# Order and size of the loads in the last stage of a long-convolution and mixture-of-experts kernel: x requested ahead of z, z in two halves, the last z stores on ScalarE's queue

## The chip, the cores and the metric

The kernel runs on one core of a Trainium2 chip. The metric is the device time of the whole program in microseconds (us), which is better when lower. A core has TensorE (PE, with its weight loads shown apart as PEld), VectorE (DVE), ScalarE (ACT), GpSimd (POOL) and SyncE (SP), each with its own instruction stream, and 16 DMA engines that they share. SP does no arithmetic here: it waits on semaphores and issues most of the DMAs, strictly in program order.

## The reference

The reference is a gated long convolution followed by a sparse layer of experts:

```python
h_filt = (np.maximum(pos_emb @ w1, 0) @ w2) * exp(-0.01 * pos)[:, None]
u = x * v
y = irfft(rfft(u, 2S) * rfft(h_filt, 2S), 2S)[:, :S]      # causal convolution, S = 11456, 4 batches, 128 channels
t = (x * y).reshape(B * S, D)                             # 45824 rows of 128
do_compute = t @ w_skip > 0
e = argmax(t @ w_gate);  g = softmax(t @ w_gate)[e]       # 8 experts
out = t;  out[do_compute] += g * (relu(t @ w1[e]) @ w2[e])   # hidden size 1024
```

## The kernel before, in words

The convolution is done as a two-step Fourier transform with 60 x 64 points, with the sequence cut into three blocks (`NB = 3`) and the 128 channels into four quarters of 32. There are three stages.

- `first_phase` multiplies x by v, computes the filter, and does the first half of the forward transform. Its result goes to DRAM (`x1d`, `x1f`).
- `freq_phase` reads it back, multiplies by the filter in the frequency domain, does the first half of the inverse transform, and stores the result in DRAM as `zd`. Its `store()` (line 425) issues two DMAs of 384 KB for each finished z tile, from SP (line 429). It is called once in each turn of the loop, and once more after the loop (line 481) for the last tile.
- `out_phase`, the last stage, has 32 chunks (`NCH = 32`) of 3 blocks, so 96 blocks. For a chunk it needs a tile `zt` with its part of `zd` (1440 KB, all three blocks of it; there are `ZB = 2` such tiles), and for each block a tile `ox` with the same rows of x (256 KB, three tiles, `ZT = 3`). `product` (line 1060) does the second half of the inverse transform for one block: matmuls of `zt` into the PSUM tile `y` (line 1068; the first pair of matmuls reads rows 0 to 3 of `zt`, the second pair rows 4 to 7), then a DVE multiplication of `y` with `ox` into `xm` (line 1069). There is one `y` buffer, so the matmuls of a block wait for the multiplication of the block before.

After its product each block goes through steps that lag behind: transposes of `xm` on PE (`turn`), the scores (`score`, `score2`), and, per chunk, the choice of the expert, counts, ranks and a list of the rows of each expert that a DMA writes to DRAM (`write`, line 1197). The block itself is stored to `out` seven steps after its product (`store`, line 1073). From about the ninth chunk on, the instructions of the first expert units (`early_slots`) are mixed in: GpSimd reads the lists and gathers rows by indirect DMAs (lines 657 and 691), PE multiplies them with the experts' weights, and GpSimd scatters the results (line 762). After the last chunk `late_slots` does the remaining units, with almost no other DMA work.

What sets the order of the work is a table written out by hand (lines 1269 to 1294): one step for each block, and in it functions sorted by a rank. Chunk 0 has steps 0 to 2, chunk 1 steps 4 to 6, chunk 2 steps 7 to 9, and from there on each chunk follows the last without a gap. Each engine gets its instructions in that order at build time, and waits only on semaphores. Within a step, a list write has rank -3, the product rank 0, and the store of an earlier block rank 9. So SP's stream in a steady chunk is: block 0 - ox, out; block 1 - list, ox, out; block 2 - zt, ox, out. An ox that is asked for at block q is the one for block q + 2, and the zt asked for at block 2 of chunk ch is the one for chunk ch + 2, which takes the tile that chunk ch has just finished with.

The change touches `store` of the second stage (lines 425 to 430 and 481), `load_z` (1046), the first loads of the last stage (1205 to 1209) and `produced` (1262), which calls the loads after each product.

Of the kernel before, what the change touches and what calls it, by code (L numbers as in the profile page):

```python
# [10 lines left out]
F32 = mybir.dt.float32  # L11
# [10 lines left out]
NB = 3  # L22
K1, N2 = 60, 64
L = K1 * N2
H2 = N2 // 2
NS = NB * B
N = L * NS
NP = 4
DH = D // NP
# [16 lines left out]
KS = 4  # L46
# [7 lines left out]
ZT = 3  # L54
ZB = 2
# [265 lines left out]
def freq_phase(tc, nc, i, fi, zd, c3, spare, loads):  # L321
# [9 lines left out]
    with (  # L331
# [90 lines left out]
                step()  # L422
            return back

        def store():
            while done_z:
                h, k, z = done_z.pop()
                for p in range(2):
                    nc.sync.dma_start(zd[p, h, :, :, KS * k:KS * k + KS].rearrange("m c k d -> (m c) k d"),
                                      z[p * 64:(p + 1) * 64].rearrange("n k s d -> n k (s d)"))  # L430

        LAG = 1
# [16 lines left out]
        for n in range(ALL + LAG):  # L449
# [17 lines left out]
            back(0)  # L467
            begin(n + 1, 0)
            store()
            if n < ALL:  # L470
                half(1)
# [5 lines left out]
            if n < ALL:  # L477
                nc.gpsimd.tensor_tensor(y[:, 1:], y[:, 1:], p1, ALU.add)  # L478
                nc.gpsimd.tensor_tensor(y[:, 2:], y[:, 2:], p2, ALU.add)  # L479
            back(2)  # L480
        store()


class Experts:
# [515 lines left out]
def out_phase(tc, i, out, zd, ex, consts):  # L1000
# [3 lines left out]
    nc = tc.nc  # L1004
    NT = NS
    NCH = H2
    with (
# [3 lines left out]
      with (  # L1011
# [21 lines left out]
        zs = zd.rearrange("p h m c k w -> m (c k) (p h) w")  # L1033
        c4s, xms, zx, zts, lgs = {}, {}, {}, {}, {}

        def load_x(q):

            ch, blk = divmod(q, NB)
            if blk == 0 and ch % C4 == 0:
                c4s[ch // C4] = ob.tile([2 * K1, C4, 2, 64], F32, name="c4", bufs=2)  # L1040
                nc.sync.dma_start(c4s[ch // C4].rearrange("p a b c -> p (a b c)"), i["c4"][ch // C4])
            x = ob.tile([128, NP, B, DH], F32, name="ox", bufs=ZT)
            nc.sync.dma_start(x, i["xo"][ch, blk])
            return x

        def load_z(ch):
            if ch < NCH:
                zts[ch] = ob.tile([2 * K1, 2 * NP, NS * DH], F32, name="zt", bufs=ZB)
                nc.sync.dma_start(zts[ch], zs[ch])

        def load(q, x=None):

            ch, blk = divmod(q, NB)
            if q >= NB * NCH:
                return
            if x is None:
                x = load_x(q)
            zx[q] = zts[ch][:, :, blk * BW:(blk + 1) * BW], x

        def product(ch, blk):  # L1060
            z, x = zx.pop(NB * ch + blk)
            if blk == 0:
                xms[ch] = ob.tile([128, NS, W], F32, name="xm", bufs=XM)
            xm = xms[ch]
            s = slice(blk * B, (blk + 1) * B)
            y = opy.tile([128, NP, B, DH], F32, name="y")
            for p in range(2):
                nc.tensor.matmul(y[p * 64:(p + 1) * 64], c4s[ch // C4][:, ch % C4, p, :], z[:, NP * p:NP * (p + 1)], start=True, stop=True)  # L1068
            nc.vector.tensor_tensor(xm[:, s, 0:D].rearrange("p b (h d) -> p h b d", h=NP), y, x, ALU.mult)  # L1069

        def store(ch, blk):
            s = slice(blk * B, (blk + 1) * B)
            ex.store_rows(nc.sync.dma_start(out[ch][:, s], xms[ch][:, s]), ch)
            if blk == NB - 1:
                del xms[ch]
# [127 lines left out]
            base += n * u  # L1203
        work = ex.early_slots(eb, ob, eps, bank[2])
        ahead = [load_x(q) for q in range(ZT - 1)]
        for ch in range(ZB):
            load_z(ch)
        for q, x in enumerate(ahead):
            load(q, x)
        tables = []  # L1210
# [50 lines left out]

        def produced(ch, blk):
            product(ch, blk)
            if blk == NB - 1:
                load_z(ch + ZB)
            load(NB * ch + blk + ZT - 1)


        first = lambda ch: START[ch] if ch < len(START) else START[-1] + NB * (ch - len(START) + 1)
# [1 line left out]
        for ch in range(NCH):  # L1271
            for blk in range(NB):
                for lag, rank, f in ((0, 0, produced), (1, 4, turn), (2, 4.9, score), (3, 2, score2), (STORE, 9, store)):
                    steps.setdefault(first(ch) + blk + lag, []).append((rank, f, (ch, blk)))
            for lag, order, f in (
                    (6, 3, choose), (7, 1, exp), (7, 4.5, count), (7, 6, counted), (7, 6, gate), (8, 4.4, total),
                    (9, -2.5, even), (9, 0.5, spreadcounts), (9, 4.5, ranks),
                    (10, -2, routed), (11, 3, spread), (12, 4.5, collect), (13, -3, write)):
                steps.setdefault(first(ch) + lag, []).append((order, f, (ch,)))
# [27 lines left out]
def program(tc, i, out):  # L1307
# [5 lines left out]
    with tc.tile_pool(name="mc", bufs=1) as mc:  # L1313
        wf = mc.tile([128, 2 * E * F], F32, name="wf")
        fi = First(nc, i, x1d, x1f, mc, wf)
        spare = wf[:, fi.used:]
        c3 = mc.tile([128, 2, 128], F32, name="c3")
        first_phase(tc, fi)
        nc.scalar.dma_start(c3, i["c3"])
        later = {}  # L1320

        def prepare():

            later["ex"] = Experts(tc, i, out, lists, mc, wf)
            yield
            later["consts"] = out_consts(nc, i, mc)
            for e in range(E):
                if e % 2 == 0:
                    yield
                later["ex"].weights(e, 0)  # L1330

            for e in range(E):
                if e != 1:
                    yield
                later["ex"].weights(e, 1)
        freq_phase(tc, nc, i, fi, zd, c3, spare, prepare())
        out_phase(tc, i, out, zd, later["ex"], later["consts"])
# [53 lines left out]
```

## Time and profile before

| What | Value |
|---|---|
| Time, median of 3 runs | 1851.17 us (1851.14 to 1859.37) |
| The profiled execution's own time | 1847.63 us |
| Its span | 1845.8 us |
| Mean granted TensorE clock over the span | 0.928 of full |
| PE busy over the span | 1613.2 us (87%) |
| `zt` loads | 32 DMAs of 1440 KB |
| `ox` loads | 96 DMAs of 256 KB |
| `out` stores of blocks | 96 DMAs of 258 KB |

The span is the time from the first to the last instruction of one profiled execution. A row of a waits view reads: the engine and line that stood idle, what ended the idle time, the sum in us, how often, and the longest. A row of a windows view reads: the stretch in us from the start of the span, its length, then for each engine the busy us and the instructions, the granted TensorE clock, the mean busy share of the 16 DMA engines, and GB/s. The time that packets overlap on one DMA engine counts twice, so that share can go a little over 1. A row of a timeline reads: start, length, engine, line, operation, out<-in, count, and in brackets the idle time of the engine before it with what ended it; rows of SP are the issues of DMAs (several of one line in a row are merged), not their transfers.

### The profile page before, as it was taken

The numbers are of one execution on the slowest core, as the hardware profiler recorded it, in microseconds if no ns is written. First come the engines' busy times: TensorE is split into PE (matmuls) and PEld (weight loads), VectorE is DVE, ScalarE is ACT, GpSimd is POOL, SyncE is SP. The second block draws the span as 40 slices with busy tenths as digits, with TensorE's granted clock in tenths as the row PEclk, the third lists the DMA queues.
The fourth block names the chain that finished last, engine by engine and source line by source line (L and its number), as shares of the span: only waits on it lengthen the run. The fifth ranks groups of instructions, "written<-read, shape, count | busy, mean of one in ns | idle before, by whom it ended". The sixth has DMA issues, their size and how long they took to land. (4 is left out here: it accounts for less than half of the span.)

```text
span 1845.8 us, 26677 instructions
## 1 busy us (share of the span) xinstructions
PE 1613.2 (87%) x8528; PEld 1002.9 (54%) x8528; DVE 1194.7 (65%) x2521; ACT 831.1 (45%) x1740; POOL 1025.5 (56%) x667
## 2 busy tenths in 40 slices
PE   6968999999999999566887968999869988899897
PEld 2533333344334444222565756666657766778896
DVE  1316777777777999436774845676656645577775
ACT  3543545444455444122443534444425534455564
POOL 1115888888887788200455243234466666666674
PEclk9987999999999999787898989999889889899899
DMA  9999999999998798789986876887211111111110
GB/s 240 324 334 280 357 346 306 346 330 304 347 318 271 225 344 229 166 196 232 220 196 159 216 179 167 207 220 194 72 25 24 34 38 37 35 36 34 31 34 19
DMA packets 209385, 353.97 MB, mean 192 GB/s; under 512 B 55146, under 2 KB 157884, under 8 KB 209244
## 3 DMA queue, kind: packets, MB, share of 16 engines
q1 hardware_dynamic: 190332, 312.99, 58.6%
q0 software_dynamic: 18144, 38.67, 7.5%
q8 instruction: 69, 1.13, 0.3%
q10 hardware_dynamic: 768, 0.59, 0.1%
q14 instruction: 72, 0.59, 0.1%
HBM read 209.12 MB, written 144.02 MB: 191 GB/s over the span
## 5 line engine op out<-in xcount | busy, mean ns | idle before, releaser
L762 POOL DMA_INDIRECT out<-o,ids x186 | 206.0, 1107 | 316.0 <-DVE o L768 254.1
L418 PE MATMUL zps<-y,c 128*128 128x512 f32 x720 | 336.6, 597 | 1.8 <-POOL y L478 1.4
L478 POOL TENSOR_TENSOR y<-y,p 128x2048 f32<-128x2048 f32 x60 | 271.9, 4532 | 65.6 <-DVE p L407 65.1
L691 POOL DMA_INDIRECT xt<-out,ids x186 | 201.7, 1084 | 96.6 <-issue 53.3
L866 DVE SCALAR_TENSOR_TENSOR hh<-hp,hh 128x1024 fp32r<-128x1024 f32 x128 | 155.9, 1218 | 124.8 <-ACT hh L865 66.0
L418 PEld LDWEIGHTS zps<-y,c 128*128 128x128 f32 x720 | 134.5, 190 | 171.2 <-issue 154.2
L407 DVE TENSOR_TENSOR p<-xp,g 128x1024 f32<-128x1024 f32 x240 | 217.2, 945 | 0.0
L407 DVE TENSOR_TENSOR y<-xp,g 128x1536 f32<-128x1536 f32 x120 | 210.7, 1756 | 4.1
L657 POOL DMA_INDIRECT ids<-lists,at x93 | 102.8, 1106 | 158.7 <-DVE at L652 131.2
L865 ACT ACTIVATE hh<-hp 128x1024 fp32r<-128x1024 f32 x128 | 132.0, 1032 | 121.4 <-PE hp L758 60.2
L419 ACT COPY z<-zps 128x512 f32<-128x512 f32 x180 | 105.6, 587 | 167.4 <-PE zps L418 162.9
L1068 PE MATMUL y<-zt,c 120*64 120x512 f32 x384 | 117.0, 691 | 51.1 <-DVE xm L1069 24.5
L733 DVE TENSOR_TENSOR ws<-wf,ws 128x1024 fp32r<-128x1024 f32 x113 | 137.6, 1218 | 16.2 <-issue 9.8
L1069 DVE TENSOR_TENSOR xm<-y,ox 128x512 f32<-128x512 f32 x96 | 66.1, 689 | 126.1 <-PE y L1068 53.8
L756 PE MATMUL hp<-hl,ws 128*128 128x512 f32 (+1 forms) x336 | 127.7, 380 | 19.5 <-issue 10.7
L479 POOL TENSOR_TENSOR y<-y,p 128x1024 f32<-128x1024 f32 x60 | 141.7, 2362 | 4.7
L218 ACT COPY wf<-ps 120x384 f32<-120x384 f32 x256 | 110.0, 482 | 70.1 <-PE ps L216 70.1
L216 PE MATMUL ps<-wf,c 60*120 60x384 f32 x512 | 126.0, 563 | 13.1 <-POOL wf L199 7.2
L828 PEld LDWEIGHTS bank<-wd,h 128*128 128x128 f32 x928 | 116.8, 205 | 34.0 <-issue 34.0
L828 PE MATMUL bank<-wd,h 128*128 128x128 f32 x928 | 127.4, 294 | 0.4 <-issue 0.4
L387 PE MATMUL xp<-x,wf 128*128 128x480 f32 x256 | 120.7, 596 | 5.5 <-issue 3.8
L199 POOL TENSOR_TENSOR wf<-wf 124x768 f32<-124x768 f32 x48 | 87.3, 1818 | 63.7 <-DMA wf<-xv 33.6
(188 smaller groups left out, 3160.8 us busy)
## 6 DMA issues: line engine op xcount, KB each, us to landing
wf<-xv SPq DMA_DIRECT2D x128, 360.0 KB
x1d<-wf SPq DMA_DIRECT2D x64, 720.0 KB
x<-x1d SPq DMA_DIRECT2D x60, 768.0 KB
zd<-z SPq DMA_DIRECT2D x120, 384.0 KB
zt<-zd SPq DMA_DIRECT2D x32, 1440.0 KB
out<-xm SPq DMA_DIRECT2D x96, 258.0 KB
ox<-xo SPq DMA_DIRECT2D x96, 256.0 KB
x1f<-fx POOLq DMA_DIRECT2D x16, 720.0 KB
```

Of the source, the lines that this page charges most:

```text
L216: nc.tensor.matmul(ps[p], self.c1[rows], u[rows, q * RUN:(q + 1) * RUN], start=True, stop=True)
L407: nc.vector.tensor_tensor(o[:, :, :, j * KH:(j + 1) * KH].rearrange("p s a k b d -> p (s a) k b d"), x[:, None].broadcast_to([128, m, KH, ...
L418: nc.tensor.matmul(zps, c3[:, a, :], y[:, blk, a], start=(a == 0), stop=(a == 1))
L478: nc.gpsimd.tensor_tensor(y[:, 1:], y[:, 1:], p1, ALU.add)
L479: nc.gpsimd.tensor_tensor(y[:, 2:], y[:, 2:], p2, ALU.add)
L691: ins = nc.gpsimd.indirect_dma_start(out=xt[:, j], out_offset=None, in_=self.rows[0:have], in_offset=bass.IndirectOffsetOnAxis(ap=ids[:, j ...
L733: eng.tensor_tensor(w[:, 1], src[:, ds(self.where(eng, tb), F)], w[:, 0].bitcast(F32), ALU.subtract)
L756: nc.tensor.matmul(hp, w[:, 0, c], hl[:, 0], start=True, stop=False)
L762: ins = nc.gpsimd.indirect_dma_start(out=self.rows, out_offset=bass.IndirectOffsetOnAxis(ap=ids[:, j:j + 1], axis=0), in_=o, in_offset=Non ...
L828: nc.tensor.matmul(bank[:, j * D:(j + 1) * D], h[f // 2][:, f % 2, j * 128:(j + 1) * 128], wd[s][:, f * D:(f + 1) * D], start=(f == 0), st ...
L865: nc.scalar.activation(h[:, 0], hp, AF.Relu)
L866: nc.vector.scalar_tensor_tensor(h[:, 1], hp, 0.0, h[:, 0].bitcast(F32), ALU.max, ALU.subtract)
```

## The change

Three things change.

- After the product of a block, the ox of block q + 2 is now asked for first, and zt after it.
- A zt load is issued as two DMAs of 720 KB, rows 0 to 3 and rows 4 to 7 of the tile. The first half for chunk ch + 2 is asked for at block 2 of chunk ch, where the whole was; the second half at block 0 of chunk ch + 1, one block later. At the start only chunk 0's halves are asked for before the first product; both halves of chunk 1 follow at block 0 of chunk 0, behind the third ox.
- The store after the loop of the second stage, two DMAs, is issued by ScalarE instead of SP.

```diff
-        def store():
+        def store(eng=nc.sync):
             while done_z:
                 h, k, z = done_z.pop()
                 for p in range(2):
-                    nc.sync.dma_start(zd[p, h, :, :, KS * k:KS * k + KS].rearrange("m c k d -> (m c) k d"),
+                    eng.dma_start(zd[p, h, :, :, KS * k:KS * k + KS].rearrange("m c k d -> (m c) k d"),
                                       z[p * 64:(p + 1) * 64].rearrange("n k s d -> n k (s d)"))
...
-        store()
+        store(nc.scalar)
...
-        def load_z(ch):
+        def load_z(ch, p):
+
             if ch < NCH:
-                zts[ch] = ob.tile([2 * K1, 2 * NP, NS * DH], F32, name="zt", bufs=ZB)
-                nc.sync.dma_start(zts[ch], zs[ch])
+                if p == 0:
+                    zts[ch] = ob.tile([2 * K1, 2 * NP, NS * DH], F32, name="zt", bufs=ZB)
+                rows = slice(p * NP, p * NP + NP)
+                nc.sync.dma_start(zts[ch][:, rows], zs[ch][:, rows])
...
-        for ch in range(ZB):
-            load_z(ch)
+        for p in range(2):
+            load_z(0, p)
...
             product(ch, blk)
+            load(NB * ch + blk + ZT - 1)
+
             if blk == NB - 1:
-                load_z(ch + ZB)
-            load(NB * ch + blk + ZT - 1)
+                load_z(ch + ZB, 0)
+            elif blk == 0:
+                if ch == 0:
+                    load_z(1, 0)
+                load_z(ch + 1, 1)
```

## The prediction

> **What bounds the kernel now.** I read the stretches of the span first, then who waited for whom, then the timelines of SP and DVE where the waits lie. The last stage by stretches:
>
> ```profile
> core 0: us, PE busy (x) PEld busy (x) DVE busy (x) ACT busy (x) POOL busy (x), PEclk, DMA share, GB/s
> 764.00:794.50 30.50, 13.87 (x71) 5.06 (x71) 4.10 (x7) 3.51 (x10) 0.00 (x0) 0.72 0.94 194
> 794.50:808.50 14.00, 8.56 (x55) 3.61 (x54) 4.90 (x17) 3.44 (x12) 0.00 (x0) 0.74 0.86 199
> 808.50:822.50 14.00, 8.63 (x57) 3.75 (x54) 7.05 (x21) 3.07 (x11) 0.00 (x0) 0.74 0.84 191
> 822.50:836.50 14.00, 8.46 (x68) 4.08 (x67) 6.35 (x25) 3.46 (x12) 0.00 (x0) 0.74 0.96 237
> 836.50:851.00 14.50, 9.05 (x72) 4.33 (x71) 9.04 (x36) 3.53 (x12) 0.00 (x0) 0.74 0.93 221
> 851.00:864.50 13.50, 9.42 (x88) 4.68 (x90) 10.62 (x48) 3.56 (x12) 0.00 (x0) 0.88 0.92 227
> 864.50:878.50 14.00, 9.18 (x75) 4.35 (x74) 9.47 (x46) 3.46 (x12) 1.25 (x2) 0.74 0.98 228
> 878.50:895.00 16.50, 12.12 (x94) 6.03 (x92) 11.16 (x48) 5.07 (x15) 7.54 (x6) 0.71 0.81 192
> ...
> 910.00:1304.00 394.00, 339.07 (x2914) 248.88 (x2912) 245.51 (x907) 176.62 (x426) 159.75 (x150) 0.94 0.78 191
> 1304.00:1400.00 96.00, 71.89 (x522) 61.70 (x521) 59.91 (x235) 36.93 (x63) 59.39 (x55) 0.84 0.14 37
> 1400.00:1838.00 438.00, 395.03 (x2199) 341.54 (x2197) 290.43 (x421) 229.16 (x282) 279.52 (x251) 0.94 0.13 33
> ```
>
> Until about 895 us no engine is near full: a chunk of about 14 us has some 9 us of PE, at a clock of 0.74, while the DMA share is 0.81 to 0.98. From 910 to 1304 it is the reverse: PE is busy 339 of 394 us at a clock of 0.94. The change moves loads, so its effect lies before 895 if anywhere. Whether loads are waited for there:
>
> ```profile
> DVE xm L1069 <- DMA ox<-xo: 40.0, 10, 6.4
> ```
>
> ```profile
> DVE xm L1069 <- DMA ox<-xo: 4.6, 4, 3.2
> ```
>
> The first row is of 773 to 912 us, the second of 912 to 1310. So the multiplication waits for x about once per chunk, some 4 us each time, and hardly ever afterwards. Why it waits, from SP and DVE:
>
> ```profile
> 793.86 0.34 SPq L1049 DMA_DIRECT2D zt<-zd  x1
> 794.29 0.96 SPq L1043 DMA_DIRECT2D ox<-xo  x2
> ```
>
> ```profile
> 804.79 0.69 DVE L1069 TENSOR_TENSOR xm<-y,ox 128x512 f32<-128x512 f32 x1 [6.44 <-DMA ox<-xo]
> ```
>
> The 256 KB of x are asked for 0.43 us after 1440 KB of z, and are used 10.5 us later. And the DMA engines then run dry, because the next z is asked for only after a product that was itself held up:
>
> ```profile
> 758.50:762.50 4.00, 0.00 (x0) 0.00 (x0) 0.00 (x0) 0.00 (x0) 0.00 (x0) 0.55 0.94 226
> 762.50:764.50 2.00, 0.00 (x0) 0.00 (x0) 0.00 (x0) 0.00 (x0) 0.00 (x0) 0.50 0.86 286
> ...
> 772.00:779.50 7.50, 5.35 (x14) 1.63 (x16) 1.38 (x2) 0.32 (x1) 0.00 (x0) 0.51 1.06 203
> ...
> 792.50:794.50 2.00, 2.00 (x8) 0.83 (x8) 0.64 (x2) 0.00 (x0) 0.00 (x0) 0.64 0.02 8
> 794.50:796.00 1.50, 1.50 (x12) 0.50 (x12) 1.33 (x7) 1.01 (x3) 0.00 (x0) 0.50 0.54 118
> 796.00:802.50 6.50, 4.10 (x36) 1.75 (x32) 1.67 (x5) 1.94 (x7) 0.00 (x0) 0.96 1.10 213
> 802.50:806.50 4.00, 0.97 (x4) 0.29 (x4) 1.21 (x5) 0.30 (x1) 0.00 (x0) 0.60 0.98 295
> 806.50:808.50 2.00, 2.00 (x9) 1.06 (x6) 0.69 (x1) 0.19 (x1) 0.00 (x0) 0.50 0.07 25
> ```
>
> Read 792.5 to 808.5 as one chunk: 2 us empty, a slow start, z at a share of 1.10, x and out at 0.98, then empty again. **So the bound before 895 is the DMA queue together with a loop: x behind z delays the product, and the late product delays the next z.**
>
> **The change, part by part.**
>
> *Order and halves.* No byte is added: 1440 KB of z, three ox and three out per chunk remain. With x ahead, the last two products of a chunk no longer stand behind a whole z; each x has at most one half ahead of it. While one z tile is being used, both halves of the next are already queued, with x and out between, so the queue holds work when the next product comes. I therefore price the stretch by the queue alone. Its work is the sum of length times share: 30.5 x 0.94 + 14 x 0.86 + 14 x 0.84 + 14 x 0.96 + 14.5 x 0.93 + 13.5 x 0.92 + 14 x 0.98 + 16.5 x 0.81 = 118.9 us, in 131 us. A queue that stays full has a share of 0.98 (x and out, 802.5 to 806.5) to 1.05 (6.5 us at 1.10 with 4 us at 0.98). That gives 121.3 or 113.2 us: a gain of 9.7 to 17.8 us. I take 1.02: 116.6 us, **14.4 us less**. The eight rows cover about nine chunks, so a chunk would take some 13 us. PE's 9 and DVE's 4 to 11 us per chunk fit in that; the ox waits that remain cost nothing extra, since the queue is what they wait for.
>
> *The last of these chunks.* Part of the hole in 878.5 to 895 is not made by x:
>
> ```profile
> 888.89 0.77 PE L745 MATMUL mh<-ident,xt 128*128 128x128 f32 x2 [4.38 <-DMA xt<-out,ids]
> ```
>
> This is the first gather of an expert unit, a chain of indirect DMAs. At 1.02 the row has 16.5 - 13.4/1.02 = 3.4 us of hole; I keep half of it: **1.7 us back** (bounds 0 and 3.4).
>
> *Price of a second DMA per z.* SP's extra issue is 0.34 us, and SP stands idle, in the mean, 7.5 and 4.4 us before issues in block 1 of a chunk:
>
> ```profile
> SPq L1197 <- DVE sel L1163: 172.9, 23, 13.5
> SPq L1073 <- DVE xm L1128: 88.8, 20, 9.8
> ```
>
> On the queue, the two 384 KB stores of zd back to back (758.5 to 762.5) lack 0.06 x 4 = 0.24 us of a full share, their start included; from below, two z DMAs one behind the other (772 to 779.5) show no hole at all. Nine extra DMAs in the stretch: 0 to 2.2 us, taken as **1 us**; later the queue has room (0.78). Below nothing is possible only as in the second rival.
>
> A rule speaks against this part. The Trainium skill (DMA: Bandwidth & Descriptors, "Rules for kernel authors") wants 1 MiB or more per DMA for full bandwidth and says that two transfers to disjoint partition halves only serialize. The halves here lie side by side in the same partitions, yet both are under 1 MiB. Its "Anatomy of one DMA" fits a fixed 2.0 us to each DMA of the GpSimd path; nine of these one after the other would be an estimated 18 us and turn the sum into a loss. The row of 772 to 779.5, with a share of 1.06, shows no such pause between queued DMAs, so I do not follow it.
>
> *The second wait.* The second pair of matmuls of a chunk's first product now waits for a half of its own:
>
> ```profile
> L1068 PEldq EVENT_SEMAPHORE  x31: 51/51/51, 773.2 to 1288.7; - x31
> ```
>
> 51 ns, on the path in the some 22 of 32 chunks after 910: **1.1 us**. Behind it on PE stand that block's product and the transposes of the one before. It should find its half there: that was asked for three blocks earlier, and with 22 chunks in the 394 us a chunk takes 17.9 us.
>
> *The start.*
>
> ```profile
> 756.92 0.59 ACT L419 COPY z<-zps 128x512 f32<-128x512 f32 x1 [1.84 <-PE zps L418]
> 757.53 1.24 SPq L429 DMA_DIRECT2D zd<-z  x2
> 758.90 1.03 SPq L1041 DMA_DIRECT2D c<-c  x1
> 759.98 2.03 SPq L1043 DMA_DIRECT2D ox<-xo  x2
> 762.87 0.96 SPq L1049 DMA_DIRECT2D zt<-zd  x2
> 773.31 1.98 PE L1068 MATMUL y<-zt,c 120*64 120x512 f32 x4 [16.43 <-DMA zt<-zd]
> 779.18 0.59 ACT L1083 COPY xT<-tp 128x512 f32<-128x512 f32 x1 [21.68 <-PE tp L1081]
> ```
>
> SP waits for the last copy of z, stores it, and only then loads c4 and two ox; z must wait for the stores to land in any case. With the stores on ScalarE, c4 and the two ox (2 us, 762.5 to 764.5) can go before them, if their buffers are free, which no row shows. ScalarE's two issues (1.24 us on SP) stand in an idle time of 21.68 us; without that cover they would cost 1.24 us. The first pair of matmuls can start on the first half. Bounds: 0 and 2 + 2 = 4 us (both matmul pairs, 1.98, out of the way); I take **1 us gained**, near the lower end.
>
> *After 895.* The order of every engine is fixed and PE is the bound, so all later work moves with the stretch: no part is given back by rule. PE still stands idle 55 of 394 us there, in waits that the change does not touch but shifts, so 4 us either way may come of it.
>
> **Sum:** 14.4 - 1.7 - 1 - 1.1 + 1 = 11.6, so 12 us. The profiled execution took 1847.63 us (span 1845.8 and 1.8 around it) and would take 1836. It stands 3.5 us under the median of the runs, 1851.17, so I forecast **1839 us**, with 1831 to 1845 as this case's own range.
>
> **The rivals.**
>
> 1. *Fixed price per half.* The slow start in 794.5 to 796 (1.5 us at 0.54) costs 0.7 us. If each half pays it, two per chunk and nine chunks are 12.6 us less the 6.3 us paid now: gain 12 - 6 = 6 us, **1845 us**. For it: the slow start itself. Against it: the full share between two queued z. (The Trainium skill's fixed cost, above, would side with this rival.)
>
> 2. *More than the queue's sum.* The upper bounds hold: 17.8 us, 4 us at the start, no price of halves, no gather wait: about 22 us, **1829 us**. For it: the 40.0 us of waits are far above the sum. A gather, too, waits for a landing:
>
> ```profile
> 890.76 1.00 POOL L691 DMA_INDIRECT xt<-out,ids  x1 [7.67 <-DMA ids<-lists,at]
> ```
>
> If that is time behind a z, a half would shorten it. (By the Trainium skill, DMA: Bandwidth & Descriptors, "Queues, rings and completion order", an engine serves its queues in turn, a packet of up to 64 descriptors at a time, which would let a gather in between halves.) Against it: the share of 0.98 for x and out.
>
> 3. *The order does not get onto the queue.* SP's 7.5 and 4.4 us of idle time in block 1 come ahead of an x, and the holes stay. If the queue empties meanwhile, nothing is gained: **1851 us**. Against it: with both halves asked for just before block 1, some 8 us of work are queued then.
>
> 4. *Slower: the second half comes late.* It is asked for one block later than now. If, after 910, PE waits for it at each of 22 chunks, the 12 us are used up at 0.55 us per chunk, and at 1 us per chunk the kernel takes 1839 + 22 = **1861 us**. It decides once SP's hold and the queue together exceed the three blocks, 17.9 us. For it: the longest holds, 13.5 and 9.8 us. Against it: they come after the request in SP's order, and the queue is at 0.78.
>
> **How the numbers follow.** Forecast 0.52; more than the sum 0.20; fixed price 0.11; no new order 0.10; slower 0.07. A measurement of this kernel can tell about 0.5%, 9.3 us, from no change: faster is under 1841.9, slower over 1860.4. Faster: 0.40 of the forecast, 0.20, and 0.04 of the fixed price, 0.64. Slower 0.07, the rest 0.29. For the range I leave out what lies above 1852 (0.09) and below 1828 (0.09).
>
> **What would show it.** Right: between 773 and 905 the waits of line 1069 for ox shrink to well under 15 us, no 2 us windows with a share near 0 are left, a chunk takes about 13 us, the first expert unit's transposes, at 888.89, come near 877, and 910 to 1304 keeps its length. Wrong: holes of the same size (third rival), z windows with a share well under 1 (first), PE waits for zt after 910 (fourth), or a stretch after 895 that has grown by what was saved before it.

## The result

The changed kernel takes 1839.2 us (median of 12 runs, 1832.06 to 1848.6), the kernel before in the same comparison 1858.62 us (12 runs, 1851.14 to 1871.92). The ratio is 0.9905, with a 95% interval of 0.9881 to 0.9929, so 13 to 22 us of 1858.62 are gained, in the middle 17.7 us. That is more than the 0.5% which a measurement of this kernel can tell.

Of the two profiled executions, the one of before (1847.63 us) lies below all its 12 runs and the one of after (1840.31 us, span 1838.5) near its median. This pair shows only 7.3 us between them, so stages are compared one by one below.

The last stage of the changed kernel, in stretches (the columns are those of the prediction's first fence):

```profile
core 0: us, PE busy (x) PEld busy (x) DVE busy (x) ACT busy (x) POOL busy (x), PEclk, DMA share, GB/s
788.00:800.00 12.00, 9.38 (x62) 4.06 (x63) 5.61 (x17) 3.84 (x13) 0.00 (x0) 0.86 1.06 241
...
836.00:848.00 12.00, 9.78 (x59) 4.50 (x61) 7.98 (x43) 2.62 (x9) 0.00 (x0) 0.56 1.02 282
...
860.00:878.00 18.00, 11.22 (x87) 6.01 (x86) 12.75 (x54) 5.11 (x15) 6.01 (x6) 0.69 0.93 234
878.00:895.00 17.00, 15.57 (x145) 11.44 (x144) 11.22 (x42) 7.70 (x19) 6.33 (x7) 0.99 0.83 209
910.00:1296.00 386.00, 333.79 (x2826) 245.68 (x2826) 239.30 (x879) 170.34 (x414) 146.25 (x138) 0.92 0.74 185
```

The DMA share is 0.93 to 1.06 in these rows up to 878. Cut into windows of 2 us, 776 to 878 has a lowest share of 0.41, once, where before had windows of 0.02 and 0.07.

The waits of the changed kernel between 765 and 915 us, where before had 40.0 us for ox:

```profile
PE y L1071 <- DMA zt<-zd: 13.8, 4, 10.7
...
PE y L1071 <- DMA c<-c: 7.3, 2, 4.8
...
DVE xm L1072 <- DMA ox<-xo: 2.9, 3, 1.6
```

The wait for x is gone, from 40.0 to 2.9 us. Beside it stand PE's waits for z (10.7 of the 13.8 us are the first load) and, new, for c4, a small table that SP loads for two chunks at a time. What they cost is seen in the time of a chunk. Six chunks, from the first product of chunk 2 to that of chunk 8, first in before, then in after:

```profile
797.00:882.00 85.00, 54.30 (x409) 25.50 (x410) 48.78 (x195) 20.66 (x72) 4.23 (x3) 0.76 0.92 217
```

```profile
795.30:864.00 68.70, 54.89 (x418) 25.91 (x418) 48.84 (x194) 21.17 (x73) 1.73 (x2) 0.82 1.03 264
```

14.2 us per chunk became 11.45, with the same PE, DVE and ACT work in both, and 264 in place of 217 GB/s. This measure, six chunks from product to product, is used for all kernels below.

The start and the first expert, from the timeline of after:

```profile
756.11 1.74 SPq L1043 DMA_DIRECT2D ox<-xo  x2
...
760.26 0.59 ACT L419 COPY z<-zps 128x512 f32<-128x512 f32 x1 [1.84 <-PE zps L418]
760.88 1.15 ACTq L429 DMA_DIRECT2D zd<-z  x2
...
770.96 1.94 PE L1071 MATMUL y<-zt,c 120*64 120x512 f32 x2 [10.74 <-DMA zt<-zd]
...
776.52 0.69 DVE L1072 TENSOR_TENSOR xm<-y,ox 128x512 f32<-128x512 f32 x1 [17.13 <-PE y L1071]
...
872.20 1.04 PE L745 MATMUL mh<-ident,xt 128*128 128x128 f32 x2 [6.17 <-DMA xt<-out,ids]
```

SP asks for x at 756.11, ahead of the stores of z, and PE starts on the first half alone. The last copy of z (line 419), which the change does not touch, comes 3.3 us later in this execution than in before (760.26 against 756.92), so I measure from it. To the first multiplication it takes 16.26 us, where before took 775.38 - 756.92 = 18.46 us.

### The profile page after: what moved, and what is told of

The parts are those of the page before. It is cut to its first block, busy times and chain, and to the rows that moved or that the text cites. A ratio compares the mean times of both kernels' runs of the same rounds, so it can differ in the third digit from the quotient of the medians.

```text
span 1838.5 us, 26706 instructions
## 1 busy us (share of the span) xinstructions
PE 1614.4 (88%) x8528; PEld 1004.1 (55%) x8528; DVE 1195.8 (65%) x2521; ACT 831.1 (45%) x1740; POOL 1023.8 (56%) x667
## 5 line engine op out<-in xcount | busy, mean ns | idle before, releaser
L1071 PE MATMUL y<-zt,c 120*64 120x512 f32 x384 | 120.9, 690 | 27.4 <-DMA zt<-zd 13.8
L756 PE MATMUL hp<-hl,ws 128*128 128x512 f32 (+1 forms) x336 | 126.2, 376 | 20.4 <-DVE hh L866 12.9
L387 PE MATMUL xp<-x,wf 128*128 128x480 f32 x256 | 120.6, 596 | 6.0 <-issue 3.8
L728 ACT CAST ws<-wf 128x1024 fp32r x113 | 117.9, 1044 | 7.5 <-issue 2.3
```

The costliest lines, as they stand in the source:

```text
L756: nc.tensor.matmul(hp, w[:, 0, c], hl[:, 0], start=True, stop=False)
```

## The experiments

All read alike: the ratio to the kernel before on the same chip, the six chunks, and the distance from the last copy of z to the first multiplication of chunk 9, called the way to chunk 9. That way is 142.0 us in before and 121.2 us in after.

### One part of the change at a time

Four kernels ran beside one another. The first is the changed kernel again.

> The changed kernel once more. Queue theory (order and halves together keep the DMA queue full while nothing else is the bound): time 0.987 to 0.994 of the kernel before; from the last copy of z in the second stage to the first product of chunk 9 about 121 us (142 before), share of the DMA engines 1.0 or more in between. The first profile of it lost some 9 us of that lead between 895 and 921 us. If that is a chance of one execution, the lead at chunk 11 is 16 us or more here; if it belongs to the change, it is 10 to 13 us again.

The second has the order alone: z stays whole.

```diff
         def produced(ch, blk):
             product(ch, blk)
+            load(NB * ch + blk + ZT - 1)
             if blk == NB - 1:
                 load_z(ch + ZB)
-            load(NB * ch + blk + ZT - 1)
```

> Only the order: x of the next block ahead of z, z whole, stores as before. Queue theory: one x of each chunk, the one asked for at block 0, still stands behind a whole z, so the late product only moves from block 1 to block 2 and the queue still runs dry: ratio 0.997 to 1.001, waits of the multiplication for ox of 30 us or more. Rival, the order alone does it: ratio 0.988 to 0.993 and waits under 15 us.

The third has the halves alone: each is asked for in the change's block, but still ahead of x, and at the start z of both chunks is asked for ahead of the first product, as before. `load_z` is that of the change.

```diff
             product(ch, blk)
             if blk == NB - 1:
-                load_z(ch + ZB)
+                load_z(ch + ZB, 0)
+            elif blk == 0 and ch > 0:
+                load_z(ch + 1, 1)
             load(NB * ch + blk + ZT - 1)
```

> Only the halves: z in two DMAs at the places of the change, but still ahead of x; stores and the first loads as before. Queue theory: each of two x per chunk stands behind a half, the product at block 2 comes as late as before: ratio 0.996 to 1.001. Rival, the smaller pieces alone do it: ratio 0.988 to 0.993. Rival, a half has a price of its own: ratio over 1.001.

The fourth has only the last stores of the second stage on ScalarE's queue.

```diff
-        store()
+        store(nc.scalar)
```

> Only the last two stores of z on ScalarE's queue. Both theories: c4 and two ox go ahead of the stores, the first product comes 0 to 3 us earlier after the last copy of z: ratio 0.998 to 1.000. If the start made the gain, the ratio would be under 0.995.

| kernel | median us | ratio, 95% interval | us per chunk | way to chunk 9, us |
|---|---|---|---|---|
| before | 1710.6 | | | |
| change again | 1683.86 | 0.9839 (0.9826 to 0.9853) | 11.2 | 120.4 |
| order alone | 1687.38 | 0.9856 (0.9839 to 0.9874) | 12.0 | 127.8 |
| halves alone | 1690.2 | 0.9882 (0.9866 to 0.9897) | 11.9 | 124.8 |
| store alone | 1708.84 | 0.9992 (0.9979 to 1.0005) | 14.0 | 141.1 |

The six chunks of the change again, of the order alone, of the halves alone and of the store alone:

```profile
798.00:865.20 67.20, 51.78 (x407) 23.99 (x408) 48.82 (x194) 20.89 (x71) 1.37 (x2) 0.88 1.04 269
```

```profile
804.00:875.80 71.80, 53.45 (x418) 26.17 (x419) 48.56 (x195) 21.12 (x73) 3.14 (x3) 0.82 1.05 257
```

```profile
801.60:873.00 71.40, 51.16 (x409) 24.43 (x408) 48.51 (x196) 20.85 (x72) 2.45 (x3) 0.86 1.05 260
```

```profile
797.30:881.50 84.20, 57.29 (x417) 26.71 (x417) 48.75 (x194) 21.29 (x73) 3.97 (x3) 0.75 0.92 220
```

I had reasoned that x ahead of z works through the halves, and that one without the other would leave the queue empty. That is wrong: the share is 1.05 with either edit alone, and each alone brings most of the gain. Cut into windows of 2 us, the six chunks have a lowest share of 0.94 with the order alone and 0.98 with the halves alone, where the store alone has 0.10. The two gains do not add, since both fill the same holes. With both, the rate in the profiles is 269 GB/s against 257 and 260. In time the change is clearly ahead of the halves alone, but not clearly of the order alone, whose four runs (1682.77 to 1694.7 us) overlap with those of the change (1680.49 to 1684.68 us). The stores on ScalarE's queue change nothing that can be measured by themselves.

The waits for x, in the order alone and in the halves alone, 765 to 915 us:

```profile
DVE xm L1069 <- DMA ox<-xo: 24.9, 9, 5.2
```

```profile
DVE xm L1071 <- DMA ox<-xo: 27.0, 11, 3.7
```

Some two thirds of the wait are still there (33.1 us in the store alone, 37.3 and 40.0 us in two profiles of before) while the loss is nearly gone; both kernels lie between the 30 us and the 15 us that the expectations had. So the 40 us of before were not what was lost; what was lost was the empty queue that the late product caused.

Which product is late decides that. One chunk of before, then one of the order alone:

```profile
818.68 0.69 DVE L1069 TENSOR_TENSOR xm<-y,ox 128x512 f32<-128x512 f32 x1 [5.24 <-DMA ox<-xo]
...
819.43 1.98 PE L1068 MATMUL y<-zt,c 120*64 120x512 f32 x4 [5.37 <-DVE xm L1069]
...
822.21 0.39 SPq L1049 DMA_DIRECT2D zt<-zd  x1
```

```profile
818.52 1.08 PE L1068 MATMUL y<-zt,c 120*64 120x512 f32 x4
...
821.54 0.47 SPq L1049 DMA_DIRECT2D zt<-zd  x1
...
824.46 0.69 DVE L1069 TENSOR_TENSOR xm<-y,ox 128x512 f32<-128x512 f32 x1 [3.82 <-DMA ox<-xo]
```

In before the x that is late is that of the second block. The third block's matmuls wait for its multiplication, because there is one `y`, and z waits for those matmuls, which are the last to read its tile. With the order alone the late x is that of the third block. Its multiplication still waits 3.82 us, but its matmuls are done, so the next z is asked for 2.92 us ahead of it and the queue stays full.

### Is it the queue, and is there a price per DMA?

Four kernels ran on another chip (kernel before: 1881.15 us). The first is the kernel before with z whole and in the old order, but issued by ScalarE.

```diff
-                nc.sync.dma_start(zts[ch], zs[ch])
+                nc.scalar.dma_start(zts[ch], zs[ch])
```

> The kernel before with one edit: z, whole and in the old order, is issued by ScalarE, so it is in a DMA queue of its own and no x stands behind it in SP's. Theory that x is late because it stands behind z in one queue: the waits for ox fall under 15 us and the ratio is 0.985 to 0.995 (a loss of a few us is possible where ScalarE stands before the issue until the product's matmuls are done). Rival, the DMA engines are simply shared and x comes as late from any queue: waits of 30 us or more and a ratio of 0.998 or more.

The second is the changed kernel without the second half of z: the first half is used in its place, so it moves 720 KB less per chunk, and the choice of experts and with it the later stages differ.

```diff
-                rows = slice(p * NP, p * NP + NP)
-                nc.sync.dma_start(zts[ch][:, rows], zs[ch][:, rows])
+                rows = slice(0, NP)
+                if p == 0:
+                    nc.sync.dma_start(zts[ch][:, rows], zs[ch][:, rows])
```

> The changed kernel without the second half of z: it is not loaded, and both pairs of matmuls read the first half, so the outputs and what is routed to the experts differ and only the stretch before the experts is compared. If the DMA queue is the bound there, a chunk loses some 4 us until PE or DVE bounds it: 8.5 to 10.5 us a chunk in chunks 2 to 7 instead of 12.5, first product of chunk 9 some 95 us after the last copy of z. If PE, DVE or waits between the engines were the bound, a chunk stays at 12 us or more.

The third issues each half as two DMAs of 360 KB in the same place; the fourth is the kernel before.

```diff
-                rows = slice(p * NP, p * NP + NP)
-                nc.sync.dma_start(zts[ch][:, rows], zs[ch][:, rows])
+                for r in range(p * NP, p * NP + NP, NP // 2):
+                    rows = slice(r, r + NP // 2)
+                    nc.sync.dma_start(zts[ch][:, rows], zs[ch][:, rows])
```

> The changed kernel with each half of z as two DMAs, one behind the other at the same place. Theory that a DMA in a full queue costs next to nothing more: within 0.3% of the changed kernel (ratio to before 0.987 to 0.995), chunks 2 to 7 at 12 to 13 us. Rival, a fixed price of 0.7 us or more per DMA: 1.4 us more per chunk, 12 us in the stretch, ratio to before 0.995 to 1.0.

> The kernel before once more, for a second profile: ox waits of the multiplication 40 to 50 us, first product of chunk 9 about 142 us after the last copy of z. What of the time after chunk 9 differs from the first profile is the chance of an execution.

The six chunks of z on ScalarE's queue, of half of z, of the quarters, and of before on this chip:

```profile
799.90:871.20 71.30, 51.59 (x407) 23.62 (x408) 48.50 (x195) 20.76 (x71) 1.29 (x2) 0.79 1.00 253
```

```profile
787.40:845.20 57.80, 47.75 (x413) 23.10 (x411) 48.81 (x196) 20.71 (x72) 4.16 (x4) 0.92 0.90 248
```

```profile
791.60:857.10 65.50, 49.23 (x418) 23.58 (x418) 48.32 (x194) 21.51 (x73) 2.35 (x3) 0.92 1.04 285
```

```profile
801.20:885.10 83.90, 57.31 (x417) 26.47 (x418) 48.71 (x194) 21.24 (x73) 4.11 (x3) 0.75 0.92 219
```

- **Half of z** (one run, 1873.16 us, whose later stages are not comparable): 9.6 us per chunk, 1.3 us less than the 10.9 of the quarters on the same chip, although PE, DVE and ACT have their work unchanged; the way to chunk 9 is 99.1 us. The changed kernel itself did not run on this chip; on the others its chunk takes 10.8 to 11.45 us. So bytes hold the chunk there, but not far down: a quarter of the bytes less gave 1.3 us, not the 4 that were expected, and the share falls to 0.90, so near 9.6 us per chunk something other than the queue begins to hold.
- **Quarters**: 1854.54 us, ratio 0.9856 (0.9783 to 0.9929). The chunk of 10.9 us lies under the 12 to 13 that were expected, and the rate is the highest so far. The rival's loss from a fixed price per DMA does not show. Whether quarters beat halves cannot be read here, since the halves did not run on this chip.
- **z on ScalarE's queue**: 1866.45 us, ratio 0.9921 (0.9863 to 0.9978). The waits for x fall from 37.3 (kernel before, this chip) to 15.8 us, just above the 15 that were expected, so much of x's wait did come from standing behind z in SP's own queue. This is no pure test of the queue, since the times of issue shift too: x was asked for 0.43 us behind z in before, here 1.65 us ahead of one z (803.89 and 805.54) and 1.41 us behind another (829.96 and 831.37). But PE now waits 30.5 us for z, of which 17.3 is the first load; before had 16.8 in all.

From z on ScalarE's queue and from the kernel before on this chip, 765 to 915 us:

```profile
PE y L1068 <- DMA zt<-zd: 30.5, 5, 17.3
...
DVE xm L1069 <- DMA ox<-xo: 15.8, 5, 4.4
```

```profile
DVE xm L1069 <- DMA ox<-xo: 37.3, 9, 6.0
PE y L1068 <- DMA zt<-zd: 16.8, 1, 16.8
```

### Do quarters beat halves, and does the late c4 cost anything?

The changed kernel waits 7.3 us for c4, more than for x. c4 is asked for two blocks ahead, in a queue that is now full. The last four kernels cross the two sizes with an earlier c4, with five rounds on one chip (kernel before: 1711.0 us). The first is the changed kernel, the second the quarters of above. The third, with quarters, and the fourth, with halves, ask for c4 at block 0 of the even chunk before; the core of their edit is

```diff
-            if blk == 0 and ch % C4 == 0:
-                c4s[ch // C4] = ...
+        def load_c(ch):
+            if ch < NCH and ch % C4 == 0:
+                c4s[ch // C4] = ...
...
             elif blk == 0:
                 if ch == 0:
                     load_z(1, 0)
+                load_c(ch + 2)
                 load_z(ch + 1, 1)
```

> The changed kernel again, on a chip of its own call, beside which the next three are read. A ratio of 0.983 to 0.991 against the kernel before, as in the two comparisons so far (0.9905 and 0.9839). In chunks 2 to 7 a chunk takes 11.2 to 11.5 us, and PE waits once or twice for c4 (longest 3 to 5 us) between the last z copy and chunk 9.

> Each half of z as two DMAs of 360 KB, at the place of the half. Theory A (the full queue is priced by its bytes and no price hangs on a DMA): the same as the halves, ratios within 0.002 of one another, chunks within 0.2 us. Theory B (a smaller piece leaves less in front of x, list and out, so that the products come more evenly): some 0.4 us per chunk less, as in the single look (10.92 us a chunk), in eight chunks 3 us, a ratio 0.002 lower than the halves'. Theory C (a price per DMA of 0.3 us or more): two more per chunk in 32 chunks, but only the nine of the full queue count: 5 us or more, a ratio 0.003 higher.

> Quarters, and c4 asked for at block 0 of the even chunk before instead of two blocks ahead. If the waits for c4 are on the path (theory B'), they go, two waits of 2 to 5 us, and the ratio is 0.002 to 0.004 below that of the quarters. If they only stand where PE would wait for z anyway, because the queue is the bound (theory A), the waits go and appear as waits for z of the same sum, and the ratio stays within 0.002.

> Halves as in the changed kernel, with c4 asked for at block 0 of the even chunk before. As for the quarters: waits for c4 near 0; ratio within 0.002 of the halves' if the queue is the bound (theory A), 0.002 to 0.004 below it if the late c4 held the path (theory B').

| kernel | median us (lowest to highest) | ratio, 95% interval | way to chunk 9, us |
|---|---|---|---|
| halves (the change) | 1683.91 (1681.63 to 1686.19) | 0.9846 (0.9823 to 0.9869) | 119.6 |
| quarters | 1676.67 (1675.54 to 1681.58) | 0.9813 (0.9788 to 0.9837) | 113.4 |
| quarters, early c4 | 1676.87 (1673.36 to 1680.08) | 0.9797 (0.9772 to 0.9821) | 114.0 |
| halves, early c4 | 1683.78 (1680.98 to 1685.73) | 0.9841 (0.9819 to 0.9864) | 120.6 |

The six chunks of the halves and of the quarters:

```profile
797.60:862.60 65.00, 52.59 (x407) 24.60 (x408) 48.48 (x195) 20.88 (x71) 1.64 (x2) 0.84 1.04 276
```

```profile
792.90:857.10 64.20, 49.78 (x416) 24.14 (x417) 48.45 (x194) 21.37 (x73) 2.24 (x3) 0.90 1.04 288
```

Quarters are faster by 7.2 us, and by 6.9 us with the early c4; each time all runs of the quarters lie below all runs of the halves. So quarters beat halves with either place of c4. The profiled pair shows 6.2 us on the way to chunk 9 and 5.8 us at the end, twice what theory B had. Where they are gained, one profile of each can't tell: up to the first product of chunk 2, in the next six chunks and in chunk 8 this pair shows 3.5, 0.7 and 2.0 us, and the pair with the early c4 0.5, 4.8 and 1.4 us; the six chunks of the change alone took 68.7, 67.2 and 65.0 us in its three profiles.

c4's lateness costs nothing. The waits of the halves (760 to 905 us), and then those of the halves with early c4:

```profile
PE y L1071 <- DMA zt<-zd: 12.3, 3, 10.5
...
PE y L1071 <- DMA c<-c: 8.9, 2, 5.1
```

```profile
PE y L1073 <- DMA zt<-zd: 19.9, 9, 10.4
```

With the early c4 no row of that view has a wait for c4, and PE's wait for z has grown by 7.6 us in its place, as theory A said. Behind the full queue of this stage, which load PE waits for is only a matter of which comes last.

## Why the prediction was right, and where it was not

**The bound** was right. The order alone and the halves alone each break the loop in another way, and with each the queue's holes and most of the loss go. The half of z shows that what is left is bytes: taking some away shortens a chunk, with the work of PE, DVE and ACT as it was.

**Order and halves** had the right mechanism and an under-sized term. The prediction added up length times share, 118.9 us of work, and divided by a full share of 1.02. The holes did go. But the step took share for work, and that failed: the same bytes need less busy time when the queue is full. Six chunks in before move 217 GB/s at a share of 0.92, which is 236 at a share of 1; in after it is 264/1.03 = 256, in the quarters 288/1.04 = 277. The predicted chunk of 13 us came out at 11.45 in the first pair, and at 10.8 (halves) and 10.7 (quarters) on the last chip. Not even z and x one after the other, each at the rate of its row in the prediction, give this: 1440 KB at 213 GB/s (before, 796 to 802.5) and six transfers of x and out, 1542 KB, at 295 GB/s (802.5 to 806.5) make 6.9 + 5.4 = 12.3 us. So it seems that z and the others gain from being in flight together, which the finer pieces allow more of. That is argued from the rates; no run separates it, and the cause of the higher rate stays open. The way to chunk 9 got 20.8 us shorter in the first pair and 20.7 between the change again and the store alone, where the sum had 14.4 - 1.7 - 1 + 1 = 12.7. Up to chunk 9 the second rival, with 17.8 + 4 = 21.8 us, was the nearer one.

What I had expected of the single edits, that x needs the halves to get past z, fell with them.

**The first gather** is still late: its transposes, at 872.20 instead of the predicted 877, wait 6.17 us where they waited 4.38. So a hole stays there. The term of 1.7 us kept half of it; chunk 8, in which it lies, took 17.0 us before (881.95 to 898.96) and takes 17.4 after (864.03 to 881.47), so nothing of the 3.4 us was gained and the upper bound was the nearer one.

**The price of a second DMA** was taken as 1 us. No price is seen: halves alone gain 1.2%, and quarters gain another 7 us on the change. If a DMA has one, it is smaller than what the finer pieces gain. The Trainium skill (DMA: Bandwidth & Descriptors, "Rules for kernel authors") asks for 1 MiB or more per DMA and advises one transfer in place of two to partition halves. Here, with smaller loads queued behind, the traffic with z in DMAs of 360 KB ran at 285 and 288 GB/s and that with the whole z at 217 to 220, so the measurement goes against the size of that rule for this use; its second row, on partition halves, is not tested by a cut along the row.

**The second wait**, 1.1 us, does not exist as an instruction of its own. Line 1071 of after has as many as before, 31:

```profile
L1071 PEldq EVENT_SEMAPHORE  x31: 51/51/4797, 770.9 to 1280.4; - x31
```

Where the second half is late, the wait ends on the matmuls themselves: of the 13.8 us for z above, three waits before 905 us (1.56, 0.63 and 0.92 us) are for a second half. They fall in the stretch that the queue bounds. The 4797 ns are not a wait for z. They lie ahead of the first product of chunk 6, whose c4 SP asks for at 830.07:

```profile
830.07 0.36 SPq L1041 DMA_DIRECT2D c<-c  x1
```

```profile
L1071 PEldq EVENT_SEMAPHORE  x1: 4797/4797/4797, 833.4 to 833.4; - x1
```

By the semaphores in the trace this wait ends at 838.17, when the last part of that c4 has landed (838.13).

**The fourth rival**, a late second half after 910, did not come: from 905 to 1296 no row of the waits view of after has PE waiting for z. One row there names z, and it misleads:

```profile
971.17 0.36 SPq L1052 DMA_DIRECT2D zt<-zd  x1
...
972.54 0.92 SPq L1052 DMA_DIRECT2D zt<-zd  x1
...
1000.89 0.44 PE L745 MATMUL mh<-ident,xt 128*128 128x128 f32 x2 [1.36 <-ACT h L779]
1001.25 1.96 PE L1071 MATMUL y<-zt,c 120*64 120x512 f32 x4
...
1003.28 0.69 DVE L1072 TENSOR_TENSOR xm<-y,ox 128x512 f32<-128x512 f32 x1 [4.46 <-DMA zt<-zd]
```

This is the first block of chunk 15. Counted from the start, the 64 issues of z give its halves at 971.17 and 972.54, some 29 us ahead. DVE's 4.46 us end when PE's matmuls of that block are done, and PE came to those only at 1001.25, after other work and a wait for `h`.

**The start** gained 2.2 us where 1 was taken, near the middle of the bounds of 0 and 4.

**After 895** the shift was not carried whole in the first pair. From the first product of chunk 9 to the last product, before took 1303.96 - 898.96 = 405.0 us and after 1296.13 - 881.47 = 414.7: 9.7 us of the lead are given back, more than the 4 us allowed. PE's waits there for ScalarE's `h`, in before (899 to 1304) and in after (881.5 to 1296):

```profile
PE mh L745 <- ACT h L779: 25.2, 9, 8.7
...
PE mh L756 <- ACT h L779: 8.9, 2, 7.0
```

```profile
PE mh L745 <- ACT h L779: 29.6, 10, 9.4
...
PE mh L756 <- ACT h L779: 15.7, 6, 5.0
```

34.1 us became 45.3. On the chip of the single edits the same stretch is 343.3 us for the store alone and 339.6 us for the change: nothing is given back there (at chunk 11 the lead is still 20.4 us), and the whole gain is 1710.6 - 1683.86 = 27 us. On the chip of the half of z, which is as slow as the first, it took 428.0 us in before, 437.2 with quarters and 428.9 with z on ScalarE's queue, so there one kernel gives back 9 us and the other 1. In the first pair the profiled execution of before lies 11 us under the median of its kernel, about as much as is given back. So these single profiles do not show that the change causes it, and why PE waits longer for `h` in the first pair is open.

**The sum.** 12 us were forecast, 17.7 (13 to 22) came, between the forecast and the second rival's 22. That the time still came out at 1839 rests on two errors that offset each other: the gain was priced 6 us too low, and the base, the median of the three runs shown, 1851.17, lies 7.5 us under the median of twelve. From that median the same sum would have given some 1847 us, above the range of 1831 to 1845: that the time fell into the range is luck, while the way it was gained is not. Of the other rivals, the loss of the fixed price is ruled out by the quarters, and the order that does not reach the queue by the share of 1.03 in after and 1.05 in the order alone.

## What to carry to other kernels

A load that the next step needs should stand ahead of a large one in the same queue, or the large one should be cut, and here either alone brought most of the gain: what has to be kept is not the single wait short but the queue full. Follow a late product to the next large load: it costs only where that load has to wait for it. When pricing a fuller queue, use bytes and the rate of mixed traffic, since busy share times length is not a fixed amount of work. Once the queue is full, the waits that remain in front of it, here 7 to 9 us for c4, can be left alone, and finer pieces are worth a try on the bound itself.

## What was not expected of the hardware

The same kernel takes quite different times on different chips: the changed one 1839.2 us in the first comparison and 1683.86 and 1683.91 us on two other chips; the kernel before 1858.62, 1881.15, 1710.6 and 1711.0 us. The first 760 us are alike (last copy of z at 757 to 766 us in every profile); the last stage differs. The change on the chip of the single edits, 910 to 1220 us:

```profile
910.00:1220.00 310.00, 304.59 (x2771) 224.94 (x2771) 233.28 (x855) 167.11 (x406) 145.71 (x138) 1.00 0.90 229
```

PE is busy 98% of that stretch at a granted clock of 1.00. The same work, from chunk 9 to the last product, first in the first pair's after, then here:

```profile
881.50:1296.00 414.50, 356.15 (x3016) 262.62 (x3017) 253.99 (x936) 182.14 (x442) 161.55 (x153) 0.93 0.75 187
```

```profile
882.00:1222.00 340.00, 332.90 (x3020) 245.99 (x3019) 253.97 (x938) 182.18 (x441) 161.13 (x153) 1.00 0.90 229
```

Both the clock and idle time count. PE is busy 23 us longer at the clock of 0.93 than at 1.00, and it is idle 58 us against 7, with 45.3 us of waits for `h` in the rows above against 0.7 us here. ScalarE itself waits there for something that the trace only calls remote; before (899 to 1304):

```profile
ACT h L779 <- remote: 20.6, 7, 6.8
```

No such row stands in that stretch of the store alone or of the change again. What ScalarE waits for, no run here settles. The gain of the change held wherever it ran beside before, 1.0% in the first comparison and 1.5 to 1.6% on the two other chips, which is why kernels are compared here only with those on the same chip.
